# A fixed beat for the maxima's tiles, filter pieces in three spots, edge transposes elsewhere, and last rows asked for early, in a spectral and feed-forward kernel

## The chip, the cores and the metric

The kernel runs on one core of a Trainium2 chip. The core has five engines, each with a queue of its own that is worked off strictly in order: TensorE (PE, matmuls), VectorE (DVE), ScalarE (ACT), GpSimd (POOL) and SyncE (SP). An engine that waits for one instruction waits with everything behind it. DMAs are issued from the queues of SP, ACT and POOL and run on 16 DMA engines. On-chip data lies in SBUF (128 partitions), results of matmuls in PSUM banks. The metric is the device time of one execution in microseconds (us); lower is better.

## The reference

```python
x = A_x                                    # 1 x 2048 x 1024, float32
xn = _layernorm(x, axis=-1)
X = jnp.fft.rfft2(xn, axes=(-2, -1))
s = jnp.fft.irfft2(X * (w_r + 1j * w_i), s=(2048, 1024), axes=(-2, -1))
h = _silu(xn @ w1)                         # w1: 1024 x 3584
g = _silu(h @ w2)                          # w2: 3584 x 1024
return x + s * g
```

The global filter `w_r`, `w_i` is 2048 x 513; the two Fourier transforms are done as matmuls with constant matrices. To keep float32 accuracy on f16 matmuls, every operand is split into a high and a low f16 half, and each product is three matmuls (high·high, high·low, low·high). The splits need a scale, and the scales need maxima of the absolute values of `w1`, `w2`, `w_r` and `w_i`, so each of these is read once for its maximum.

## The kernel before

PE goes through these stages. All positions below are in us from the start of the profiled span.

1. *Plain hidden products* (L601), until 374: `xn @ w1` for the first eight pairs of 128 columns of `w1` (q < 8).
2. *The seven-product part* (L639), 374 to 617: the other six pairs (q = 8 to 13), each for two halves g of the rows, are done by Strassen's scheme. One unit (q, g) is seven products M1 to M7 of 12 matmuls 128x512, 84 products in all. Each product is followed by its evacuation from PSUM. M1, M6, M7 and M4 accumulate one after the other in the same bank, `pa`: between them ACT copies `pa` out (L651 after M1, L653 after M6, L655 after M7), and the next of them can't start on PE before that copy. M3 of a unit stands between M1 and M6 of the next.
3. *The second matrix* (L745 to L747, bank `pb`), from 617 on: seven products m = 0 to 6, each in eight parts j = 0 to 7 of 42 or 21+21 matmuls. The Fourier stages stand between them: forward (`fx`, L1200 to L1202, 16 steps u = 0 to 15), the edge column (`eps`, L1341 to L1343: nine groups of small f32 matmuls that transpose and reverse, 18 records), the filter, inverse (L1467, L1496). For m = 6 each part j finishes rows of the output: DVE L805 and L806 add the stored partial sums, ACT applies silu, L819 and L820 form s·g + x (`finish_out`), and a DMA stores it.

*What sets the order.* The program is written out by hand in one order by Python generators, and each `yield` marks the end of a slot. After every product, `after()` first writes the evacuation of the product before, then runs one slot each of `wq` (`weights1`, w1's maxima and splits), `xq` (`w2max_gen`), `yq` (`wmax_gen`) and up to three slots of the background queue `bg`, which holds the Fourier stages. So an empty `yield 0` in one of these moves what follows it by one product. What a slot writes goes into the in-order queues of SP, ACT, DVE and POOL.

In the seven-product part three streams look for maxima, all fed by DMAs on SP:

- `weights1`: the two tiles of a pair of w1 columns (`r`, L405, 512 KB each) are loaded, and some slots later ACT sums their absolute values (`magnitude`, L289). Then comes the split into f16 halves (ACT L267, DVE L270).
- `w2max_gen`: w2 tiles (`xn`, L469). ACT takes the magnitude of the even tile, DVE subtracts its two halves (L481), SP stores the difference to DRAM (`ws`, L483), and ACT takes the odd tile. In this part it has two spots in the buffer X1; a spot that a store reads can be loaded again only once the store has landed.
- `wmax_gen`: 36 pieces 128x456 of `w_r` and `w_i` (L1133) in two spots, each reduced by DVE to a maximum (L1126). The load of piece k waits for the reduce of piece k − 2.

*The edge.* `f_gen` calls the generator `edge_gen` step by step. Its first step has POOL copy the edge column into order (12 copies, L1334 to L1337), the second does the `eps` matmuls. `eps` takes a buffer from the ring "ft" of two PSUM buffers that also holds `fx`; `pb` goes through the ring "ff" of four banks (`pf`).

*The last rows.* For m = 6, `load_parts` (L738) loads the two stored partial sums of part j (`pd`), and `acc` asks by `rows_for` (L759) for four pieces 128x512: the two halves of s (`sd`) and of x. They are asked for when part j has been written, and used one part later; the last eight pieces (parts 6 and 7) are asked for after PE's part 6.

Of the kernel before, what the change touches and what calls it, by code (L numbers as in the profile page):

```python
# [10 lines left out]
F32 = mybir.dt.float32  # L11
# [8 lines left out]
NFT = F // 128  # L20
# [121 lines left out]
def spectral_ffn(ctx, tc, x, w_r, w_i, w1, w2, ca, kc, ci, tw, pm, out):  # L142
# [29 lines left out]
    def small(name, n=1):  # L172
        return sm.tile([128, n], F32, name=name)
# [113 lines left out]
    def magnitude(raw, out):  # L287
        for k in range(2):
            nc.scalar.activation(junk, raw[:, 512 * k:512 * k + 512], AF.Abs, accum_out=out[:, k:k + 1])  # L289

    def weights1():
# [105 lines left out]
        for q in range(NPL, NP):  # L397
# [7 lines left out]
                    nc.sync.dma_start(r[i], w1v[:, :, (2 * q + i) * 128:(2 * q + i + 1) * 128])  # L405
            else:
                r = early
            yield 0
            yield 0
            yield 0  # L410
            for i in range(2):
                magnitude(r[i].rearrange("p a b -> p (a b)"), ma[:, 2 * i:2 * i + 2])
                yield 0
# [45 lines left out]
    def w2max_gen():  # L459

        tiles, state = {}, [0, 0]

        def load():
            n = state[0]
            if n < NFT and n - state[1] < aux[1] and not (hold_x[0] and n % 2 == 0):
                tiles[n] = aux[0].tile([128, 2, 512], F32, name=f"w2m{n}", tag="x", bufs=4)
                for k, h in enumerate(((0, 1), (1, 0))[n % 2]):
                    f = (n & -2) + k
                    nc.sync.dma_start(tiles[n][:, k], w2[f * 128:(f + 1) * 128, h * 512:(h + 1) * 512])  # L469
                state[0] += 1  # L470
            live_x[0] = state[0] - state[1]

        for n in range(0, NFT, 2):
# [254 lines left out]
    rows = {}  # L728
    READS = ((), (), (), (), (1, 0), (), (2, 0))

    def load_parts(m, j):
# [386 lines left out]

    def wmax_gen():

        mt, tl = small("mw", 36), []
        spots = Map({"y": [(R2[0], 72 * KB + 256), (R2[0], 74 * KB + 256)]})

        def reduce():
            k, t_ = tl.pop(0)
            nc.vector.tensor_reduce(mt[:, k:k + 1], t_, axis=AX.X, op=OP.max, apply_absolute_value=True)  # L1126

        for k in range(36):
            if len(tl) == 2:
                reduce()  # L1130
            src = (w_r, w_i)[k // 18].rearrange("(p r) k -> p (r k)", p=128)
            tl.append((k, spots.tile([128, 456], F32, name=f"wm{k}", tag="y")))
            nc.sync.dma_start(tl[-1][1], src[:, 456 * (k % 18):456 * (k % 18 + 1)])  # L1133
            yield 0.6
            if k % 3 == 2:
                yield 0
        yield 0
        while tl:
            reduce()
# [49 lines left out]
    def f_gen():  # L1189
# [56 lines left out]
        for u in range(16):  # L1246
# [73 lines left out]
    def edge_gen():  # L1320
# [15 lines left out]
            g.tensor_copy(r0[:, n, 0], xv[:, n, 0, 0])  # L1336
            g.tensor_copy(r0[:, n, 1:4], xv[:, n, 0, 3:0:-1])  # L1337
        yield 1
        ps = P["t"].tile([128, 1024], F32, name="eps", tag="ft")
        for n in range(3):  # L1340
            nc.tensor.matmul(ps[:, n * 32 + 8:n * 32 + 32], perm[:, 0], rv[:, n, 1:4].rearrange("m q a r -> m (q a r)"), start=True, stop=True)  # L1341
            nc.tensor.matmul(ps[:, n * 32:n * 32 + 8], perm[:, 1], rv[:, n, 0].rearrange("m a r -> m (a r)"), start=True, stop=False)
# [290 lines left out]
    with tc.manual_schedule():  # L1633
# [168 lines left out]
        for n, (m, j, k) in enumerate(steps):  # L1802
# [77 lines left out]
```

## Time and profile before

| | us |
|---|---|
| three runs | 1300.14, 1294.84, 1294.86; median 1294.86 |
| the profiled execution | 1292.91 |
| its span | 1291.1 |
| PE busy | 1242.7 (96%) |
| DVE / ACT / POOL busy | 991.6 / 567.6 / 279.3 |
| L639, the seven-product part: 1008 matmuls | first at 374.18, PE idle before them 17.4 |
| last stage from 617.19 | 673.9 |

In the profile, a row names line, engine, operation and tiles (out<-in). A row "PE fx L1200 <- DVE xn L1295: 2.9, 1, 2.9" says that PE's instructions of line 1200 that write `fx` waited 2.9 us in all, in one wait, 2.9 us the longest, until DVE's instruction of line 1295 that writes `xn` was done. In a row of the timeline, "x12" merges 12 like instructions, the brackets hold the idle time before them and its releaser. "SPq" is SP's queue of DMA issues. A window's row lists the busy time and the count of each engine in turn, then the granted clock of TensorE (1.00 is full speed), the DMA engines' busy share and GB/s.

### The profile page before, as it was taken

Reading aid. Unit: us, or ns where it says so; the run is one execution under the profiler, and the core shown is the slowest. Engines: PE = TensorE matmul, PEld = TensorE weight load, DVE = VectorE, ACT = ScalarE, POOL = GpSimd, SP = SyncE. Lnnn points to the kernel's source line nnn. Section 1 sums busy time; section 2 is a strip of 40 time slices with the busy share of each in tenths; the row PEclk is TensorE's granted clock in tenths of the full one; section 3 lists DMA queues with packets and bytes.
Section 4 is the critical chain, followed back from the end, with each engine's and each line's share of the span. In section 5 each row is a group of like instructions: output and inputs, shape, how many; then the busy total and the mean of one; then the engine's idle time right before and its main releaser. Section 6 shows DMA issues by size and latency. Waiting matters only on the chain.

```text
span 1291.1 us, 18582 instructions
## 1 busy us (share of the span) xinstructions
PE 1242.7 (96%) x6827; PEld 643.3 (50%) x6827; DVE 991.6 (77%) x1628; ACT 567.6 (44%) x844; POOL 279.3 (22%) x428
## 2 busy tenths in 40 slices
PE   8999999999998988999999999999979999999996
PEld 5544444444443433444445455555544456566654
DVE  6678998899986776785478949996798347886774
ACT  4854575655456676755333223332323222422211
POOL 1211242533441222312300000202125200110011
PEclk9999999999999898999999999999989999999998
DMA  7569697858578788837855788989999988888587
GB/s 241 128 160 231 160 313 204 257 139 216 131 201 230 253 248 277 243 89 239 284 176 184 225 272 200 312 239 301 216 298 266 356 314 321 290 294 283 188 288 233
DMA packets 181595, 306.68 MB, mean 238 GB/s; under 512 B 31744, under 2 KB 89856, under 8 KB 180352
## 3 DMA queue, kind: packets, MB, share of 16 engines
q1 hardware_dynamic: 135584, 163.85, 42.1%
q0 software_dynamic: 30128, 92.82, 25.4%
q10 hardware_dynamic: 15792, 48.83, 10.7%
q8 instruction: 53, 0.87, 0.3%
q14 instruction: 38, 0.31, 0.1%
HBM read 204.25 MB, written 111.67 MB: 245 GB/s over the span
## 4 chain that ended last, share of the span: by engine, by line
PE 50%; DMA 10%; DVE 6%; issue 4%; ACT 3%; POOL 1%; SPq 0%; ACTq 0%; DVEq 0%; POOLq 0%
PE pb L745 11%; PE pb L746 11%; PE pb L747 11%; PE pa L639 5%; DMA r<-in_B_w_dram 3%; PE id L1496 3%; PE iu L1467 3%; PE pe L639 2%; DMA xn<-in_B_w_dram 2%; DMA ws<-xn 1%; DMA r<-in_A_w_r_dram 1%; PE pc L639 1%; PE fx L1200 1%; DMA hd_one<-hoone 1%; ACT both L289 1%
## 5 line engine op out<-in xcount | busy, mean ns | idle before, releaser
L601 PE MATMUL pa<-xn,w 128*128 128x512 f16 x1536 | 335.4, 380 | 5.8 <-DVE w L270 2.4
L745 PE MATMUL pb<-r,w 128*128 128x512 f16 (+1 forms) x798 | 300.3, 376 | 0.0
L746 PE MATMUL pb<-r,w 128*128 128x512 f16 (+1 forms) x798 | 300.0, 376 | 0.0
L747 PE MATMUL pb<-r,w 128*128 128x512 f16 (+1 forms) x798 | 300.0, 376 | 0.0
L601 PEld LDWEIGHTS <-w 128*128 128x128 f16 x1536 | 150.2, 98 | 186.9 <-issue 4.2
L639 PEld LDWEIGHTS <-w 128*128 128x128 f16 x1008 | 100.1, 99 | 142.9 <-issue 27.7
L747 PEld LDWEIGHTS <-w 128*128 128x128 f16 x798 | 78.2, 98 | 91.7 <-issue 1.0
L639 PE MATMUL pa<-r,w 128*128 128x512 f16 x432 | 105.7, 397 | 17.4 <-ACT h L655 8.3
L745 PEld LDWEIGHTS <-w 128*128 128x128 f16 x798 | 78.4, 98 | 85.7 <-issue 0.6
L746 PEld LDWEIGHTS <-w 128*128 128x128 f16 x798 | 78.2, 98 | 85.7 <-issue 0.6
L267 ACT ACTIVATE r<-r,sc 128x512 f16<-128x512 f32 x88 | 61.0, 715 | 99.8 <-DMA r<-in_B_w_dram 64.5
L270 DVE SCALAR_TENSOR_TENSOR r<-r,sc 128x512 f16<-128x512 f32 x88 | 64.5, 744 | 33.2 <-ACT r L267 33.2
L685 POOL DMA_DIRECT2D hd_one<-hoone x52 | 47.2, 907 | 185.1 <-DVE hoone L270 88.9
L685 POOL DMA_DIRECT2D hd_sum<-hosum x52 | 42.5, 924 | 158.8 <-DVE hosum L270 90.0
L270 DVE SCALAR_TENSOR_TENSOR hoone<-h,hs,hoone 128x2048 f16<-128x2048 f32 x28 | 65.7, 2346 | 8.0 <-ACT hoone L267 8.0
L267 ACT ACTIVATE hoone<-h,hs 128x2048 f16<-128x2048 f32 x28 | 55.9, 1995 | 15.6 <-DMA hd_one<-hoone 10.1
L267 ACT ACTIVATE hosum<-hr,hs 128x1536 f16<-128x1536 f32 x28 | 43.9, 1569 | 28.1 <-DVE hr L692 21.3
L611 ACT ACTIVATE h<-pa,ep 128x512 f32<-128x512 f32 x64 | 43.1, 676 | 29.4 <-PE pa L601 27.6
L270 DVE SCALAR_TENSOR_TENSOR hosum<-hr,hs,hosum 128x1536 f16<-128x1536 f32 x28 | 50.7, 1812 | 4.8 <-ACT hosum L267 4.8
L1200 PE MATMUL fx<-xn 128*128 128x256 f16 x192 | 44.6, 278 | 4.4 <-DVE xn L1295 2.9
L691 DVE TENSOR_TENSOR hr<-h 128x1024 f32<-128x1024 f32 x28 | 34.1, 1219 | 18.9 <-ACT h L611 14.0
L1496 PE MATMUL id<-xn 128*128 128x256 f16 x384 | 44.5, 273 | 0.0
(288 smaller groups left out, 2049.6 us busy)
## 6 DMA issues: line engine op xcount, KB each, us to landing
w<-hd_dif ACTq DMA_DIRECT2D x32, 448.0 KB, 7.3
r<-in_B_w_dram SPq DMA_DIRECT2D x56, 256.0 KB, 8.3
w<-hd_sum ACTq DMA_DIRECT2D x32, 448.0 KB, 5.8
w<-hd_one ACTq DMA_DIRECT2D x32, 448.0 KB, 6.7
hd_sum<-hosum POOLq DMA_DIRECT2D x52, 256.0 KB, 5.0
hd_one<-hoone POOLq DMA_DIRECT2D x52, 256.0 KB, 4.6
hd_dif<-hoone POOLq DMA_DIRECT2D x52, 256.0 KB, 4.3
xn<-in_B_w_dram SPq DMA_DIRECT2D x40, 256.0 KB, 4.3
```

What stands on the lines that cost most here:

```text
L267: nc.scalar.activation(hi, raw, AF.Copy, scale=scale)
L270: nc.vector.scalar_tensor_tensor(lo, raw, scale, hi, op0=OP.mult, op1=OP.subtract)
L601: nc.tensor.matmul(ps, w[:, wh, d], xt[:, xh, d], start=(n == 0), stop=(n == 23))
L611: nc.scalar.activation(hq[:, 2 * (c % 2) + f % 2], ps, AF.Silu, scale=ep[:, q:q + 1])
L639: nc.tensor.matmul(ps, lhs(d, wh), rhs(d, xh), start=(name in ("M1", "M5") and d + n == 0), stop=(d + n == 5), skip_group_check=True)
L685: defer(1, lambda k=k, m=m: stores[0].dma_start(hd[m, g][:, :, q].rearrange("f p h s -> f p (h s)"), o[:, k].rearrange("f p h s -> f p (h ...
L745: nc.tensor.matmul(ps, hh[:, 0], w[:, 0], start=first, stop=False)
L746: nc.tensor.matmul(ps, hh[:, 0], w[:, 1], start=False, stop=False)
L747: nc.tensor.matmul(ps, hh[:, 1], w[:, 0], start=False, stop=last)
L1200: nc.tensor.matmul(o, k[:, c, kh, 1], v[:, c, vh], start=(n == 0), stop=False)
L1467: nc.tensor.matmul(ps[:, q], lhs, rhs, start=(n == 0 and r == 0), stop=(n == 2 and r == 1))
L1496: nc.tensor.matmul(o, us[g][:, uh, 2 * p + r], C["ci"][:, ch, g, r], start=(n == 0 and r == 0), stop=(n == 2 and r == 1))
```

## The change

Five edits, in the order of the diff:

- `weights1`: four empty slots instead of three between the load of a pair's w1 tiles and its magnitudes.
- `w2max_gen`: in the seven-product part (where `aux[1]` is 2) a fixed pattern of six slots a pair: load of the odd tile; magnitude of the even one; subtract; store and magnitude of the odd tile; an empty slot; load of the next even tile. Before, a pair took five slots there, and the next even tile was asked for one slot after the store.
- `wmax_gen`: 54 pieces 128x304 in three spots instead of 36 pieces 128x456 in two. One load in each slot; a piece is reduced two slots after its load, and its spot is loaded again one slot after that.
- The edge: the second step of `edge_gen` from within `f_gen` comes only from u = 14 on, and `eps` takes a bank of the ring "ff".
- `load_rest`, new: as soon as, in m = 6 from j = 4 on, the background queue is empty, all rows and partial sums of the parts after the next are asked for at once, into the free buffer X1. `load_parts` and `acc` then find them there.

```diff
@@ weights1
-            yield 0
-            yield 0
-            yield 0
+            for _ in range(4):
+                yield 0
             for i in range(2):
                 magnitude(r[i].rearrange("p a b -> p (a b)"), ma[:, 2 * i:2 * i + 2])
                 yield 0
@@ w2max_gen
+        def put(n):
+            tiles[n] = aux[0].tile([128, 2, 512], F32, name=f"w2m{n}", tag="x", bufs=4)
+            for k, h in enumerate(((0, 1), (1, 0))[n % 2]):
+                f = (n & -2) + k
+                nc.sync.dma_start(tiles[n][:, k], w2[f * 128:(f + 1) * 128, h * 512:(h + 1) * 512])
...
         for n in range(0, NFT, 2):
-            while n + 1 not in tiles:
+            while n + 1 not in tiles and aux[1] == 4:
                 load()
                 yield 0
-            load()
+            early = aux[1] == 4
+            if early:
+                load()
+            elif n not in tiles:
+                put(n)
+                yield 0
+            if n + 1 not in tiles:
+                put(n + 1)
+                yield 0
             d_, o_ = tiles.pop(n), tiles.pop(n + 1)
-            magnitude(d_.rearrange("p a b -> p (a b)"), w2m[:, 2 * n:2 * n + 2])
+            size(n, d_)
             yield 0
             nc.vector.tensor_tensor(d_[:, 0], d_[:, 0], d_[:, 1], op=OP.subtract)
             yield 0.7
             nc.sync.dma_start(ws[n // 2], d_[:, 0])
-            yield 0
-            magnitude(o_.rearrange("p a b -> p (a b)"), w2m[:, 2 * n + 2:2 * n + 4])
-            state[1] += 1
-            load()
-            if aux[1] == 2:
+            if early:
                 yield 0
-            state[1] += 1
-            load()
-            load()
+            size(n + 1, o_)
+            state[1] += 2
+            if early:
+                load()
+                load()
+            else:
+                yield 0
+                yield 0
+                if n + 2 < NFT:
+                    put(n + 2)
             yield 0
@@ load_rest (new), load_parts
+    room = Map({k: [(X1, a * KB + 2 * KB * i) for i in range(n)] for k, a, n in (("rows", 24, 12), ("pt", 48, 6))})
+
+    def load_rest(j):
+        if bg_done[0] or not tdone[0] or queues["bg"]:
+            return
+        bg_done[0] = True
+        while deferred:
+            tick(False)
+        for i in range(j, 8):
+            c, p = 2 * (i // 4), i % 4
+            for _, h in FINALS[6]:
+                if (c, p, h) not in rows:
+                    rows[c, p, h] = rows_for(c, p, h, room, (("rows", 12), ("rows", 12)))
+            for k in READS[6]:
+                if (k, i) not in part:
+                    part[k, i] = room.tile([128, 512], F32, tag="pt")
+                    nc.sync.dma_start(part[k, i], pd[k, i])
...
     def load_parts(m, j):
+        if (READS[m] or (0,))[0] and (READS[m][0], j) in part:
+            return
@@ wmax_gen
-        for k in range(36):
-            if len(tl) == 2:
-                reduce()
-            src = (w_r, w_i)[k // 18].rearrange("(p r) k -> p (r k)", p=128)
-            tl.append((k, spots.tile([128, 456], F32, name=f"wm{k}", tag="y")))
-            nc.sync.dma_start(tl[-1][1], src[:, 456 * (k % 18):456 * (k % 18 + 1)])
-            yield 0.6
-            if k % 3 == 2:
-                yield 0
...
+        for k in range(57):
+            if k >= 3:
+                nc.vector.tensor_reduce(mt[:, k - 3:k - 2], tl.pop(k - 3), axis=AX.X, op=OP.max, apply_absolute_value=True)
+            yield 0.5
+            if k < 54:
+                src = (w_r, w_i)[k // 27].rearrange("(p r) k -> p (r k)", p=128)
+                tl[k] = view(R2[0], 72 * KB + 256 + 1216 * (k % 3), [128, 304], F32)
+                nc.sync.dma_start(tl[k], src[:, 304 * (k % 27):304 * (k % 27 + 1)])
@@ f_gen
-            if u >= 13:
+            if u >= 14:
                 next(edge, None)
             yield 2.5
@@ edge_gen
-        ps = P["t"].tile([128, 1024], F32, name="eps", tag="ft")
+        ps = pf.tile([128, 512], F32, name="eps", tag="ff")
@@ second matrix
+            if m == 6 and j >= 4:
+                load_rest(j + 1)
             if m == 6 or (m, j) == (5, 7):
                 load_parts(6, (j + 1) % 8)
             after(acc(m, j, banks.pop((m, j))))
```

Three places where the order of instructions moves. The first is SP's queue in the seven-product part, between two stores of w2 halves (`ws_140`, `ws_141`); `in_A_w_r_dram` are filter pieces, `in_B_w_dram` at L469 (L473 after the change) tiles of w2, at L405 of w1. Before:

```order
L483 DMA ws_140<-xn 128x512
L1133 DMA r_2498<-in_A_w_r_dram 128x456
L469 DMA xn<-in_B_w_dram 128x512 x2
L1133 DMA r_2498<-in_A_w_r_dram 128x456
L469 DMA xn<-in_B_w_dram 128x512 x2
L1133 DMA r_2498<-in_A_w_r_dram 128x456 x2
L405 DMA r_2498<-in_B_w_dram 128x8x128 x2
L483 DMA ws_141<-xn 128x512
```

And after, where the lines are L496, L1167, L473 and L405:

```order
L496 DMA ws_140<-xn 128x512
L1167 DMA r_2498<-in_A_w_r_dram 128x304 x2
L473 DMA xn<-in_B_w_dram 128x512 x2
L1167 DMA r_2498<-in_A_w_r_dram 128x304
L473 DMA xn<-in_B_w_dram 128x512 x2
L1167 DMA r_2498<-in_A_w_r_dram 128x304 x2
L405 DMA r_2498<-in_B_w_dram 128x8x128 x2
L1167 DMA r_2498<-in_A_w_r_dram 128x304
L496 DMA ws_141<-xn 128x512
```

The first reload after a store stands two products behind it instead of one, and six filter pieces stand between two stores instead of four.

The second place is PE around the edge's transposes, before the change; `fx_8121` is step u = 14 of the forward transform, and `pb_7` the next part of the second matrix:

```order
L1202 LDWEIGHTS xn
L1202 MATMUL fx_8121<-xn 128x128
L1341 MATMUL eps<-xn 128x24
L1342 MATMUL eps<-xn 128x8
L1343 MATMUL eps<-xn 128x8
L745 LDWEIGHTS w_67
L745 MATMUL pb_7_8193<-r_2498,w_67 128x512
```

After the change (`fx_8285` is step u = 15, and `pb_0` the part behind `pb_7`), the three rows of `eps` standing three times in a row in both kernels:

```order
L1230 LDWEIGHTS xn
L1230 MATMUL fx_8285<-xn 128x128
L1369 MATMUL eps<-xn 128x24
L1370 MATMUL eps<-xn 128x8
L1371 MATMUL eps<-xn 128x8
L783 LDWEIGHTS w_67
L783 MATMUL pb_0_8350<-r_2498,w_67 128x512
```

The transposes moved from behind u = 14 to behind u = 15, with the 42 matmuls of `pb_7` and all of u = 15 now ahead of them.

The third place is the end of SP's queue, in m = 6, from the partial sums of part 6 on (`pl_6`, `pd_6`); `sd_1` and `fs_1`, `fx_1` are the rows of part 5, `sd_2` those of part 6, `sd_3` of part 7. Before:

```order
L738 DMA pl_6_2_10883<-pd_6_118 128x512
L738 DMA pl_6_0_10885<-pd_6_102 128x512
L759 DMA fs_1_1_10887<-sd_1_129 128x512
L759 DMA fx_1_1_10889<-in_A_x_dram 128x512
L759 DMA fs_1_0_10891<-sd_1_129 128x512
L759 DMA fx_1_0_10893<-in_A_x_dram 128x512
L738 DMA pl_7_2_10948<-pd_7_119 128x512
L738 DMA pl_7_0_10950<-pd_7_103 128x512
L759 DMA fs_2_1_10952<-sd_2_130 128x512
L759 DMA fx_2_1_10954<-in_A_x_dram 128x512
```

After, from the partial sums of part 6 on (the rows `sd_2` of part 6 stand just ahead of these):

```order
L763 DMA xn<-pd_6_118 128x512
L763 DMA xn<-pd_6_102 128x512
L797 DMA xn<-sd_3_131 128x512
L797 DMA xn<-in_A_x_dram 128x512
L763 DMA xn<-pd_7_119 128x512
L763 DMA xn<-pd_7_103 128x512
L797 DMA fs_1_1_10929<-sd_1_129 128x512
L797 DMA fx_1_1_10931<-in_A_x_dram 128x512
L797 DMA fs_1_0_10933<-sd_1_129 128x512
L797 DMA fx_1_0_10935<-in_A_x_dram 128x512
```

The 12 loads of parts 6 and 7 (each pair `sd_3`, `x` stands twice) now come ahead of the four of part 5, which were third in the list before.

More of the change, by code (lines that the diff above doesn't have):

```diff
@@ L464, in load, with size @@
             n = state[0]
[L465 to L469, printed above, removed]
+            if n < NFT and n - state[1] < 4 and aux[1] == 4 and not (hold_x[0] and n % 2 == 0):
+                put(n)
                 state[0] += 1
             live_x[0] = state[0] - state[1]
+        def put(n):
[3 more added lines that the diff above has]
+                nc.sync.dma_start(tiles[n][:, k], w2[f * 128:(f + 1) * 128, h * 512:(h + 1) * 512])
+        def size(n, t_):
+            magnitude(t_.rearrange("p a b -> p (a b)"), w2m[:, 2 * n:2 * n + 2])
         for n in range(0, NFT, 2):
-            while n + 1 not in tiles:
+            while n + 1 not in tiles and aux[1] == 4:
                 load()
                 yield 0
-            load()
+            early = aux[1] == 4
+            if early:
+                load()
+            elif n not in tiles:
+                put(n)
+                yield 0
+            if n + 1 not in tiles:
+                put(n + 1)
+                yield 0
             d_, o_ = tiles.pop(n), tiles.pop(n + 1)
-            magnitude(d_.rearrange("p a b -> p (a b)"), w2m[:, 2 * n:2 * n + 2])
+            size(n, d_)
             yield 0
@@ L729, in spectral_ffn @@
     READS = ((), (), (), (), (1, 0), (), (2, 0))
+    room = Map({k: [(X1, a * KB + 2 * KB * i) for i in range(n)] for k, a, n in (("rows", 24, 12), ("pt", 48, 6))})
[14 more added lines that the diff above has]
+                    nc.sync.dma_start(part[k, i], pd[k, i])
+    bg_done = [False]
     def load_parts(m, j):
+        if (READS[m] or (0,))[0] and (READS[m][0], j) in part:
+            return
         while m == 6 and held.get("pt"):
@@ L1119, in wmax_gen @@
     def wmax_gen():
[L1121 to L1126, printed above, removed]
-        for k in range(36):
-            if len(tl) == 2:
-                reduce()
-            src = (w_r, w_i)[k // 18].rearrange("(p r) k -> p (r k)", p=128)
-            tl.append((k, spots.tile([128, 456], F32, name=f"wm{k}", tag="y")))
-            nc.sync.dma_start(tl[-1][1], src[:, 456 * (k % 18):456 * (k % 18 + 1)])
-            yield 0.6
-            if k % 3 == 2:
-                yield 0
-        yield 0
-        while tl:
-            reduce()
+        mt, tl = small("mw", 54), {}
+        for k in range(57):
[6 more added lines that the diff above has]
+                nc.sync.dma_start(tl[k], src[:, 304 * (k % 27):304 * (k % 27 + 1)])
         m = small("mwx")
```

## The prediction

> **What bounds the kernel now.** I read the page's busy line first, then what PE waits for in its groups of instructions, then its timeline.
>
> ```profile
> span 1291.1 us, 18582 instructions
> PE 1242.7 (96%) x6827; PEld 643.3 (50%) x6827; DVE 991.6 (77%) x1628; ACT 567.6 (44%) x844; POOL 279.3 (22%) x428
> ```
>
> PE is busy for 96% of the span, and the change neither adds nor removes a matmul. So it can gain only what PE waits, what PE loses at a lower clock, and what follows PE's last matmul. The costliest wait of PE's groups in 374 to 618 us is this one (count, busy time and mean ns, then idle time before it and its releasers):
>
> ```profile
> L639 PE MATMUL pa<-r,w 128*128 128x512 f16 x432 | 105.7, 397 | 17.4 <-ACT h L655 8.3 <-ACT pc L651 6.0 <-ACT h L653 3.1
> ```
>
> L639 is the seven-product part: 17.4 us, all of it for ACT to read bank `pa`. PE's timeline shows the undisturbed beat and the four large ones (a row is start, duration, then in brackets the idle time before it and its releaser):
>
> ```profile
> 374.18 2.75 PE L639 MATMUL pa<-xn,w 128*128 128x512 f16 x12
> ...
> 385.86 2.75 PE L639 MATMUL pc<-xn,w 128*128 128x512 f16 x12
> 388.45 2.75 PE L639 MATMUL pa<-r,w 128*128 128x512 f16 x12
> ...
> 404.41 2.75 PE L639 MATMUL pa<-r,w 128*128 128x512 f16 x12 [2.85 <-ACT h L653]
> ...
> 421.95 5.10 PE L639 MATMUL pa<-r,w 128*128 128x512 f16 x12 [4.43 <-ACT pc L651]
> ...
> 457.14 4.44 PE L639 MATMUL pa<-r,w 128*128 128x512 f16 x12 [4.19 <-ACT h L655]
> ...
> 499.76 5.28 PE L639 MATMUL pa<-r,w 128*128 128x512 f16 x12 [4.14 <-ACT h L655]
> ...
> 617.19 0.38 PE L745 MATMUL pb<-r,w 128*128 128x512 f16 x1
> ```
>
> A product takes 388.45 − 385.86 = 2.59 us, so 84 of them take 217.6 us. The part lasts 617.19 − 374.18 = 243.0 us. **25.4 us are lost**: the four large waits are 2.85 + 4.43 + 4.19 + 4.14 = 15.6 us, the small ones the other 1.8, and the last 8.0 is a slower clock, since after the three waits of over 4 us a product takes 4.4 to 5.3 us instead of 2.75.
>
> ACT isn't late from work but from waiting in order. At the third wait, SP's and ACT's timelines read:
>
> ```profile
> 447.69 2.55 SPq L405 DMA_DIRECT2D r<-in_B_w_dram  x2
> 455.13 0.63 ACT L289 ACTIVATE both<-r 128x512 f16<-128x512 f32 x1 [7.26 <-DMA r<-in_B_w_dram]
> 456.51 0.58 ACT L655 ACTIVATE h<-pa 128x512 f32<-128x512 f32 x1
> ```
>
> A magnitude (L289) stands in ACT's queue ahead of the evacuation L655, waits 7.26 us for its w1 tile, and PE waits for L655. The tile was late at its source: its load was issued by SP behind filter pieces, only at 447.69. ACT's and SP's waits from 366 to 605 us say how often:
>
> ```profile
> ACT both L289 <- DMA xn<-in_B_w_dram: 13.3, 8, 4.6
> ACT both L289 <- DMA r<-in_B_w_dram: 12.8, 4, 7.3
> SPq L1133 <- DVE mw L1126: 44.0, 20, 5.8
> SPq L469 <- DMA ws<-xn: 23.9, 7, 5.1
> ```
>
> SP stands 44 us for spots that the reduces haven't freed, and 24 us for a stored half to land before its spot is loaded again. Everything behind is issued late.
>
> **The change part by part.** *The fixed beat of the w1 and w2 tiles, and the filter pieces,* have one answer. Counts: as many tile loads, stores and magnitudes as before; 54 filter pieces for 36, so 18 more DMAs on SP and 18 more reduces on DVE. Landing times in 374 to 530 us (count, KB, median us from issue to landing), the slowest store, from the chain of waits, and the reduce:
>
> ```profile
> xn<-in_B_w_dram SPq DMA_DIRECT2D x38, 256.0 KB, 4.3
> r<-in_A_w_r_dram SPq DMA_DIRECT2D x18, 228.0 KB, 5.5
> r<-in_B_w_dram SPq DMA_DIRECT2D x8, 512.0 KB, 6.8
> ws<-xn SPq DMA_DIRECT2D x9, 256.0 KB, 4.7
> 386.08 8.81 DMA ws<-xn
> L1126 DVE TENSOR_REDUCE mw<-r 128x1 f32<-128x456 f32 x36 | 22.2, 622 | 17.3 <-DMA r<-in_A_w_r_dram 10.4 <-DMA r<-in_A_w_i_dram 6.8
> ```
>
> The new places in time: a store gets two products (5.2 us) until its spot is loaded again instead of one (2.6), against a median of 4.7 us; the tile that is loaded there gets two products until its magnitude, as before, against 4.3; a w1 tile gets three always (7.8 us) instead of two in three rounds of four, against 6.8. A filter piece gets two products until its reduce, and its spot one more until it is loaded again. So the medians now fit where one of them didn't, and SP's 44 us of waiting should go, since a load no longer follows at once on a reduce that DVE has yet to reach. The tails do not all fit. I keep the small waits (1.8) and, an estimate, 3.6 us for late w1 tiles: four of them, each landing in 8.7 us, 1.9 above its median. That leaves 5.4 of 25.4, a **gain of 20**. The upper bound is 24.5, with half the small waits left; the lower is 8, if nothing but the slower clock goes.
>
> The 18 more reduces: a 304-wide one lies between 0.62 × 304/456 = 0.41 us (by width; then 54 cost what 36 did) and 0.62 us (by instruction; 54 × 0.62 − 22.2 = 11.3 us more). I take the middle, +6. The sum of the windows of the part shows what hides it:
>
> ```profile
> sum 243.00, PE 225.57 PEld 100.07 DVE 175.19 ACT 159.38 POOL 65.60; mean PE 25.06 PEld 11.12 DVE 19.47 ACT 17.71 POOL 7.29
> ```
>
> DVE is free for 243 − 175 = 68 us of the part; were that cover gone, up to 11 us would be on the path. The 18 more DMAs cost SP no more than half the 2.55 us of the row at 447.69 each, for two, in which a wait is counted too: 23 us at most, hidden by the 44 us of waits that go.
>
> [...]
>
> *The edge transposes.* They cost what stands between these rows of PE and POOL:
>
> ```profile
> 954.50 0.27 PE L1200 MATMUL fx<-xn 128*128 128x256 f16 x1
> ...
> 960.83 0.40 PE L1341 MATMUL eps<-xn 128*128 128x24 f32 x2 [3.52 <-POOL xn L1334]
> ...
> 964.62 0.60 PE L1343 MATMUL eps<-xn 128*128 128x8 f32 x2 [0.30 <-POOL xn L1337]
> 966.57 0.59 PE L745 MATMUL pb<-r,w 128*128 128x512 f16 x1
> 965.78 0.18 POOL L1337 COPY xn<-xsv 128x6 f32<-128x6 f32 x1
> 966.00:970.00 4.00, 4.00 (x14) 1.85 (x14) 4.00 (x9) 3.04 (x6) 0.77 (x1) 0.57 1.02 280
> ```
>
> From 960.83 − 3.52 = 957.31 to 966.57 PE does nothing but the 18 edge matmuls, 9.3 us. The clock that the waits brought down, 0.57 on the mean of the next 4 us, costs `pb` 1.5 us more: 10.8 in all. In the new order `pb_7` (42 matmuls at 2.59/12 us, 9.1 us) and u = 15 (like u = 14, 957.3 − 954.5 = 2.8 us) stand ahead, so the edge starts near 957.3 + 9.1 + 2.8 = 969.2, after POOL's last copy ends at 965.97. Unwaited it costs PE 2.2 to 4.4 us: the last eight records took 1.95 us at the lower clock, so 18 take 4.4, and about half that at full. I take 3.0: **gain 7.8**, 6.4 to 8.6. The move into the `pf` ring (4 banks) frees `fx` from a bank held by `eps`; it costs nothing as long as the `pb` in that bank has been read, which is over 9 us earlier.
>
> *The last rows.* 12 loads move ahead of the four of j = 5; none is added. The end by the chain of waits (its DMA), PE's and DVE's timelines, the page's slices and a window:
>
> ```profile
> 1277.03 8.02 DMA fx<-in_A_x_dram
> 1281.09 0.27 PE L747 MATMUL pb<-r,w 128*128 128x256 f16 x1
> 1254.10 0.69 DVE L805 TENSOR_TENSOR pl<-pl,pb 128x512 f32<-128x512 f32 x1 [3.20 <-PE pb L747]
> 1273.43 0.75 DVE L819 SCALAR_TENSOR_TENSOR pl<-fs,s_sc,pl 128x512 f32<-128x512 f32 x1
> 1285.49 0.41 DVE L805 TENSOR_TENSOR pl<-pl,pb 128x256 f32<-128x256 f32 x1
> 1287.85 0.42 DVE L820 TENSOR_TENSOR pl<-pl,fx 128x256 f32<-128x256 f32 x1
> GB/s 241 128 160 231 160 313 204 257 139 216 131 201 230 253 248 277 243 89 239 284 176 184 225 272 200 312 239 301 216 298 266 356 314 321 290 294 283 188 288 233
> 1246.00:1251.00 5.00, 5.00 (x25) 2.27 (x24) 4.84 (x9) 1.33 (x2) 1.08 (x2) 1.00 1.00 399
> ```
>
> The last row, asked for at 1277.03, lands at 1285.05, and DVE's last instruction ends at 1288.27. PE's last matmul ends at 1281.36; the last half's work on DVE, from L805 at 1285.49 to 1288.27, is 2.8 us, so if it starts 0.3 us after PE it ends at 1284.5: the most to gain is 3.8. But from 1254.1 on, 22 pieces of 256 KiB now stand in SP's queue to the last of j = 5's, and POOL stores about six: 7.3 MB. At 399 GB/s that is 18.4 us; at 283, the lowest of the six slices ahead of the last three, 25.9. I take the middle, 340 GB/s, 21.6 us. The rows of j = 5 were used at 1273.43, 19.3 us after 1254.1. So DVE starts 2.3 us later on them; the work that it then has is two rows' ends at full width (j = 5, 6; 2.85 each, two pairs of L819 and L820 at 0.75 + 0.69), two at half (1.8) and two pairs L805, L806 (0.75), 10.8 in all without waits, and it ends 32.4 us after 1254.1 instead of 34.2: **gain 1.8**, from 3.8 to a loss of 2.5.
>
> *The sum:* 20 + 7.8 + 1.8 = 29.6. The profiled execution took 1292.91 us, 1.8 outside its span; 1292.9 − 29.6 = 1263.3. The median of the runs, 1294.86, is 1.95 above it, so **1265**.
>
> **The rivals.**
> 1. *Half the stalls stay.* For it: a store took up to 8.8 us to land, and the tile loads wait behind them in SP's one queue; store (4.7) plus load (4.3) already take 9.0 of the 10.4 us, and the stage's transfers are denser by what it runs faster. Against: medians fit. Two of the four large waits (7.8) stay with half of the clock's 8.0, the small ones (1.8) and half the 3.6: 15.4 stay, 10 are gained, 1275.
> 2. *The filter pieces pace the part.* A spot's turn (load, two products, reduce, one product) is 7.77 us, 18 times. If a piece lands and is reduced in L on the mean over such a turn, the part grows by 18 × (L − 7.77): at 9.2 us its gain is gone, at 9.7 the other gains too, and from 10.1 the kernel is slower by 0.5%. At 10.5, the part costs 49 us over its bare 217.6, 1309. For it: 5.5 us is the median of the present pieces, and DVE, in order, holds every evacuation behind a late reduce. Against: the pieces are a third smaller, and 5.5 + 0.6 is under 7.77. [...]
> 3. *The edge still waits or now holds up a `pb`,* since the two rings meet: its 7.8 are lost, 1273. Against: POOL's copies end 3 us ahead of the new place.
> 4. *The change doesn't do what it says:* the order of instructions shows that it does; no chance of its own.
>
> **How the numbers follow.** My forecast 0.62, rival 1 0.20, rival 2 0.08 (0.05 of it past 10.1 us, the rest about level), rival 3 0.10. The low end is all upper bounds together, 24.5 + 8.6 + 3.8 = 36.9: 1258. Rivals 1 and 3 together, with a loss in the last rows, are 1294.9 − 10 + 2.5 = 1287; 1282 leaves that and rival 2 out, about 2 in 10 with what lies under 1258. 0.5% is 6.5 us, about what a measurement of this kernel can tell from no change. Faster by more than that: 0.62 + 0.20 + 0.10 = 0.92, less 0.06 for pairs of rivals that come together, 0.86. Within: 0.08, these and the level part of rival 2. Slower: 0.06.
>
> **What would show it.** PE's timeline: a product each 2.59 us from start to first `pb`, and no wait for the copies of `pa` over 1 us but one; ACT's wait for w1 and w2 tiles from 26 us to under 10; SP's for reduces from 44 to under 15. No idle time before the edge matmuls, and clock 1.00 around them. After PE's end no DVE wait for a row. Wrong if DVE's waits before the reduces grow past 17 us (rival 2), if SP still waits over 12 us for `ws` (rival 1), or if the end comes more than 7 us after PE's last matmul (last rows).

## The result and the profile after

| us | before | after |
|---|---|---|
| median of the runs | 1295.55 | 1275.70 |
| profiled execution | 1292.91 | 1275.51 |
| its span | 1291.1 | 1273.7 |

The ratio of the times is 0.9836, with a 95% interval of 0.9806 to 0.9866: the kernel became 1.6% faster. The forecast was 1265, 2.3% faster, with a range of 1258 to 1282. One of the four runs after the change took 1436.49 us at a granted clock of 0.849, where the other three took 1274.33 to 1275.90 at 0.993 to 0.995, and the ratio leaves it out. The profiled execution gained 17.4 us where the sum said 29.6.

I cut each trace at the same places of PE's timeline. The cuts are the first matmul of the seven-product part, the first `pb`, the start of u = 12 of the forward transform, the end of the edge or of u = 15 (whichever is later), PE's last matmul and the end of the span:

| us | before | after | gained | forecast |
|---|---|---|---|---|
| seven-product part | 243.0 | 230.0 | 13.0 | 20 |
| from `pb` to u = 12 | 309.2 | 313.1 | −3.9 | 0 |
| u = 12 to the edge's end | 53.5 | 42.4 | 11.1 | 7.8 |
| from there to PE's end | 301.5 | 307.9 | −6.4 | 0 |
| behind PE's end | 9.7 | 6.1 | 3.6 | 1.8 |

Two rows belong together. Before, a wait for the forward transform stood behind u = 12, and after it stands ahead of u = 12 (5.0 us for `xn<-vd`). So the second and third rows make 7.2 us together. The trace of before is one execution, and among the kernels with the old edge it has the shortest of these stretches: from the first `pb` to the edge's end it took 362.7 us, the four others below 365 to 368 and those with the new edge 353 to 358.

In the part, the groups of PE's and DVE's instructions (count, busy time, mean ns, then idle time before them and its releasers) and the waits of ACT and SP from 366 to 595 us now read:

```profile
L655 PE MATMUL pa<-r,w 128*128 128x512 f16 x432 | 99.1, 379 | 11.0 <-ACT pc L667 7.5 <-ACT h L669 2.0 <-ACT h L671 1.5
...
L1162 DVE TENSOR_REDUCE mw<-r 128x1 f32<-128x304 f32 x54 | 24.7, 464 | 26.2 <-DMA r<-in_A_w_i_dram 15.5 <-DMA r<-in_A_w_r_dram 10.7
```

```profile
ACT both L289 <- DMA xn<-in_B_w_dram: 10.3, 6, 4.8
ACT hoone L267 <- DVE h L710: 7.6, 5, 3.5
```

```profile
SPq L1167 <- DVE mw L1162: 32.4, 25, 6.0
...
SPq L473 <- DMA ws<-xn: 9.6, 6, 3.1
```

PE's waits in the part fell from 17.4 to 11.0 us, the longest from 4.43 to 2.71, and its mean matmul is back at 379 ns from 397: the slower clock is gone in this trace. The granted clock of the part is 1.00, and 1.00 too in the window from 534 to 538, at the longest wait; before, it was 0.53 to 0.57 in the windows at the three waits of over 4 us, 419 to 427, 457 to 461 and 498 to 505. (In four more traces with the same part, those of after_again, after_no_edge, after_no_rows and after_less_dma below, one wait near 535 us lasted 2.86 to 3.47 us instead of 2.71, and the 12 matmuls behind it took 4.1 to 4.4 us instead of 2.75.) ACT no longer waits for w1 tiles at all (12.8 us before). But DVE waits longer ahead of the reduces than before, 26.2 us instead of 17.3. And PE's largest wait is now for L667, the evacuation of M1. The timelines of DVE, ACT and PE show what stands ahead of one of them:

```profile
522.48 0.47 DVE L1162 TENSOR_REDUCE mw<-r 128x1 f32<-128x304 f32 x1 [1.60 <-DMA r<-in_A_w_i_dram]
...
524.60 1.22 DVE L710 TENSOR_TENSOR h<-h 128x1024 f32<-128x1024 f32 x1
525.85 2.00 ACT L267 ACTIVATE hoone<-h,hs 128x2048 f16<-128x2048 f32 x1 [3.54 <-DVE h L710]
...
529.79 0.62 ACT L289 ACTIVATE both<-r 128x512 f16<-128x512 f32 x1
...
532.35 0.62 ACT L289 ACTIVATE both<-r 128x512 f16<-128x512 f32 x1
...
533.72 0.58 ACT L667 ACTIVATE pc<-pa 128x512 f32<-128x512 f32 x1
534.34 2.75 PE L655 MATMUL pa<-r,w 128*128 128x512 f16 x12 [2.71 <-ACT pc L667]
```

ACT itself waits for no DMA here. DVE waited 1.60 us for a filter piece ahead of L710; before that it had been busy for some 15 us, with six more reduces among its work. ACT had to wait 3.54 us for DVE, then works without a pause until 534.3 and comes late to L667. PE started M6 at 534.34, 2.71 us late.

At the edge, PE's timeline shows the nine groups without a wait, 957.60 to 959.58:

```profile
957.60 0.35 PE L1369 MATMUL eps<-xn 128*128 128x24 f32 x2
...
959.36 0.37 PE L1371 MATMUL eps<-xn 128*128 128x8 f32 x2
959.58 0.38 PE L783 MATMUL pb<-r,w 128*128 128x512 f16 x1
```

That is 1.98 us in place of 10.8. Behind it, waits of PE have come that the kernel before didn't have:

```profile
1015.14 0.39 PE L783 MATMUL pb<-r,w 128*128 128x512 f16 x1 [1.01 <-DMA w<-hd_one]
1032.03 0.50 PE L1495 MATMUL iu<-xn 128*128 128x256 f16 x3 [0.53 <-POOL xn L1570]
1044.68 1.67 PE L1495 MATMUL iu<-xn 128*128 128x256 f16 x7 [2.70 <-DVE xn L1505]
```

The chain of waits of the same stretch (start, duration, what) runs almost only through transfers:

```profile
958.43 8.83 DMA r<-in_B_w_dram
...
968.43 8.99 DMA r<-in_B_w_dram
...
981.23 7.93 DMA r<-in_B_w_dram
...
989.24 6.10 DMA r<-in_B_w_dram
...
1001.96 9.05 DMA r<-in_B_w_dram
...
1017.53 9.99 DMA xn<-zd
...
1027.59 10.40 DMA pd<-pl
...
1042.73 0.69 DVE pl L832
```

And the windows there (after the busy times: granted clock, DMA share, GB/s) show the DMA engines full:

```profile
945.00:985.00 40.00, 40.00 (x229) 20.97 (x227) 38.88 (x67) 16.16 (x32) 13.01 (x22) 1.00 0.98 311
1000.00:1032.00 32.00, 30.49 (x141) 13.44 (x139) 8.85 (x15) 6.27 (x11) 4.23 (x15) 1.00 1.04 370
1044.00:1048.00 4.00, 3.32 (x16) 2.40 (x17) 2.89 (x8) 1.35 (x2) 0.00 (x0) 0.58 1.05 357
```

### The profile page after: what moved, and what is told of

It is laid out like the page before. It is cut to its first block, busy times and chain, and to the rows that moved or that the text cites. A ratio compares the mean times of both kernels' runs of the same rounds, so it can differ in the third digit from the quotient of the medians.

```text
span 1273.7 us, 18601 instructions
## 1 busy us (share of the span) xinstructions
PE 1234.6 (97%) x6827; PEld 640.0 (50%) x6827; DVE 992.1 (78%) x1646; ACT 565.9 (44%) x844; POOL 269.9 (21%) x428
## 5 line engine op out<-in xcount | busy, mean ns | idle before, releaser
L655 PE MATMUL pa<-r,w 128*128 128x512 f16 x432 | 99.1, 379 | 11.0 <-ACT pc L667 7.5
L701 POOL DMA_DIRECT2D hd_sum<-hosum x52 | 42.7, 932 | 158.1 <-DVE hosum L270 101.7
L267 ACT ACTIVATE hoone<-h,hs 128x2048 f16<-128x2048 f32 x28 | 55.9, 1995 | 21.7 <-DMA hd_one<-hoone 12.2
L267 ACT ACTIVATE hosum<-hr,hs 128x1536 f16<-128x1536 f32 x28 | 44.0, 1570 | 28.6 <-DVE hr L708 23.9
L1495 PE MATMUL iu<-xn 128*128 128x256 f16 x384 | 46.2, 279 | 3.2 <-DVE xn L1505 2.7
```

What stands on the lines that cost most here:

```text
L267: nc.scalar.activation(hi, raw, AF.Copy, scale=scale)
L655: nc.tensor.matmul(ps, lhs(d, wh), rhs(d, xh), start=(name in ("M1", "M5") and d + n == 0), stop=(d + n == 5), skip_group_check=True)
L701: defer(1, lambda k=k, m=m: stores[0].dma_start(hd[m, g][:, :, q].rearrange("f p h s -> f p (h s)"), o[:, k].rearrange("f p h s -> f p (h ...
L1495: nc.tensor.matmul(ps[:, q], lhs, rhs, start=(n == 0 and r == 0), stop=(n == 2 and r == 1))
```

## The experiments

The runs of the kernel before lay higher on some chips (medians 1294.9 to 1297.7), so I compare ratios to the runs beside them, and stretches of the traces. The table holds all experiments: the stretches named above, in us, with "pb–u12" for the first `pb` to u = 12, "u12–edge" for u = 12 to the edge's end, and "to PE's end" from there. There is one trace of each.

| run | ratio, 95% interval | part | pb–u12 | u12–edge | to PE's end | behind |
|---|---|---|---|---|---|---|
| before | 1 | 243.0 | 309.2 | 53.5 | 301.5 | 9.7 |
| after | 0.9836 (0.9806 to 0.9866) | 230.0 | 313.1 | 42.4 | 307.9 | 6.1 |
| only_beat | 0.9884 (0.9867 to 0.9901) | 231.3 | 311.6 | 54.4 | 301.5 | 9.2 |
| only_pieces | 0.9946 (0.9929 to 0.9964) | 240.0 | 313.3 | 51.6 | 301.5 | 8.7 |
| only_edge | 0.9939 (0.9918 to 0.9959) | 241.9 | 312.6 | 43.2 | 308.2 | 6.3 |
| only_rows | 0.9979 (0.9962 to 0.9995) | 242.8 | 315.3 | 52.3 | 301.5 | 6.5 |
| after_no_edge | 0.9883 (0.9845 to 0.9920) | 231.3 | 313.2 | 54.3 | 301.5 | 7.2 |
| after_no_rows | 0.9877 (0.9842 to 0.9912) | 232.3 | 313.7 | 43.6 | 307.4 | 8.4 |
| after_six_pieces | 0.9787 (0.9752 to 0.9822) | 224.1 | 310.2 | 42.7 | 307.5 | 6.1 |
| after_less_dma | 0.9786 (0.9746 to 0.9826) | 233.3 | 314.3 | 41.6 | 301.5 | 6.1 |
| after_again | 0.9844 (0.9826 to 0.9863) | 233.7 | 311.7 | 43.1 | 309.5 | 6.1 |
| late_w1 | 0.9841 (0.9826 to 0.9857) | 228.7 | 311.8 | 42.7 | 310.0 | 6.1 |
| at_once | 0.9830 (0.9806 to 0.9853) | 227.3 | 314.0 | 44.0 | 308.0 | 6.4 |
| both_tuned | 0.9815 (0.9791 to 0.9838) | 226.4 | 309.9 | 45.3 | 305.8 | 6.1 |

The five kernels with the part unchanged from "after" (after, after_again, after_no_edge, after_no_rows, after_less_dma) have it at 230.0 to 233.7 us, so a difference in the part counts only outside these.

**Each part of the change alone.** The edits are those of the diff above, one group at a time; a few of their lines stand for each.

only_beat:

```diff
-            yield 0
-            yield 0
-            yield 0
+            for _ in range(4):
+                yield 0
...
-            magnitude(d_.rearrange("p a b -> p (a b)"), w2m[:, 2 * n:2 * n + 2])
+            size(n, d_)
...
+                if n + 2 < NFT:
+                    put(n + 2)
```

> The kernel before with the new beat of the w1 and w2 tiles alone; filter pieces, edge and last rows as before. Theory 1 (the gain of the seven-product part comes from the beat, and the smaller pieces in three spots hold DVE up: DVE's wait ahead of the reduces grew from 17.3 to 26.2 us): 11 to 16 us faster than before, PE's waits for the copies of pa under 11 us. Rival (the beat needs the three spots, since SP still stands 44 us for reduces ahead of the tile loads): 0 to 6 us faster, SP's wait for reduces stays over 40 us and magnitudes still wait over 15 us for tiles.

The part fell by 11.7 us with the old pieces, ACT's waits for w1 tiles were gone, and the ratio stands for 15 us: theory 1 holds here, though SP still waited 49 us for reduces. PE's waits were 11.6 us against a bound of 11. DVE waited 20.4 us for the old pieces.

only_pieces:

```diff
-        mt, tl = small("mw", 36), []
+        mt, tl = small("mw", 54), {}
...
+                tl[k] = view(R2[0], 72 * KB + 256 + 1216 * (k % 3), [128, 304], F32)
```

> The kernel before with the filter pieces alone: 54 of 128x304 in three spots, one load a product. Theory 1 (the beat gains, the pieces do not): within 4 us of before, DVE's wait ahead of the reduces over 22 us. Rival (the three spots free SP's queue, and that makes the gain): 8 to 13 us faster, SP's wait for reduces falls from 44 to about 32 us.

This lay between the two: 0.5% faster, the part 3.0 us shorter. DVE's wait ahead of the reduces was the longest of all:

```profile
L1124 DVE TENSOR_REDUCE mw<-r 128x1 f32<-128x304 f32 x54 | 24.6, 463 | 31.2 <-DMA r<-in_A_w_i_dram 17.4 <-DMA r<-in_A_w_r_dram 13.5
```

It is 31.2 us, while SP's wait for reduces fell to 20.9. Both theories had half of it: the third spot frees SP and holds DVE. Together with the beat the pieces add little (231.3 to 230.0 us, inside the spread).

only_edge:

```diff
-            if u >= 13:
+            if u >= 14:
...
-        ps = P["t"].tile([128, 1024], F32, name="eps", tag="ft")
+        ps = pf.tile([128, 512], F32, name="eps", tag="ff")
```

> The kernel before with the edge's transposes alone moved and in the other ring. The transposes themselves should take 2 us of PE without a wait instead of 10.8 with their clock. Theory 1 (the stretch behind, which moves 310 to 396 GB/s, is bound by its transfers and gives the gain back): 2 to 5 us faster, with new waits of PE between 1010 and 1060 us of 3 us or more. Rival (the new waits of the changed kernel there come from something else in it): 8 to 9 us faster, no new wait of PE behind.

The traces agree with theory 1: 10.3 us less from u = 12 to the edge's end, 6.7 us more behind it, with waits for the inverse of 2.3 and 1.6 us and 0.8 for a hidden tile. The end behind PE was 6.3 us instead of 9.7, which neither expected, and the stretch ahead of u = 12 was 3.4 us longer, so that the spans of the two traces differ by 3.1 us. The ratio stands for 8 us, more than theory 1 allowed. Where the rest comes from is not shown; the traced execution of before, 1292.91 us, is faster than all 12 of its runs beside this one (1293.92 to 1300.71).

only_rows:

```diff
+    def load_rest(j):
...
+        if (READS[m] or (0,))[0] and (READS[m][0], j) in part:
+            return
...
+            if m == 6 and j >= 4:
+                load_rest(j + 1)
```

> The kernel before with the early last rows alone. Theory 1 (the end behind PE's last matmul shrinks from 9.7 to 6.1 us, as in the changed kernel): 3 to 4 us faster, nothing else moves. Rival (the end was shorter there only because the parts before it ran otherwise): under 1.5 us faster, or slower, with DVE waiting for rows of part 5.

The end shrank from 9.7 to 6.5 us, so theory 1 holds for the end; the ratio stands for 2.7 us, just under its 3 to 4. But the rival's sign came too: in DVE's timeline the rows of part 5 were late, more than the 2.3 us of the prediction:

```profile
1276.62 0.75 DVE L841 SCALAR_TENSOR_TENSOR pl<-fs,s_sc,pl 128x512 f32<-128x512 f32 x1 [5.87 <-DMA fs<-sd]
```

It cost at most 0.4 us of the end (6.5 against 6.1 in the changed kernel), as DVE then worked through with a single wait, of 0.24 us for ACT.

**Parts of the change undone.** after_no_edge:

```diff
-            if u >= 14:
+            if u >= 13:
-        ps = pf.tile([128, 512], F32, name="eps", tag="ff")
+        ps = P["t"].tile([128, 1024], F32, name="eps", tag="ft")
```

> The changed kernel with the edge's transposes put back. Theory 1 (the transfers behind the edge give most of its gain back, and the end is as short without it thanks to the early rows): 2 to 5 us slower than the changed kernel, so 16 to 18 us faster than before; the edge's own stretch some 9 us longer, the stretch from the edge to the last inverse matmul some 6 us shorter, no wait of PE for the inverse. Rival (the edge's gain is kept whole): 8 to 9 us slower than the changed kernel.

The stretch to the edge's end grew by 11.9 us and the one behind shrank by 6.4 to the bare 301.5. Net 5.5 us by these stretches, just above theory 1's 2 to 5 and well under the rival's 8 to 9. By the ratios it is 0.9883 against 0.9836, some 6 us, with intervals that just overlap. PE didn't wait for the inverse, as theory 1 said. The end was 7.2 us, not quite as short as in the changed kernel.

after_no_rows:

```diff
-            if m == 6 and j >= 4:
-                load_rest(j + 1)
```

> The changed kernel without the early last rows. Theory 1 (with the edge moved the last eight rows land in time by themselves, since the end behind PE's last matmul was 6.3 us with the edge alone): within 1 us of the changed kernel, end 6.0 to 6.5 us. Rival (the early rows make the short end): 2.5 to 3.6 us slower than the changed kernel, end over 8.5 us.

Theory 1 falls: the end was 8.4 us, just under the rival's 8.5, and DVE waited for the last rows again. By the ratios the kernel is some 5 us slower than the changed one (0.9877 against 0.9836), with intervals that overlap; 2.3 us of that is the end. Why the end was as short as 6.3 in only_edge stays open. In every run with the early rows it is 6.1 to 7.2 us.

after_six_pieces (the maximum of the filter is taken over 6 of 54 pieces):

```diff
-            if k >= 3:
+            if 3 <= k < 9:
...
-            if k < 54:
+            if k < 6:
...
-        nc.vector.tensor_reduce(m, mt, axis=AX.X, op=OP.max)
+        nc.vector.tensor_reduce(m, mt[:, 0:6], axis=AX.X, op=OP.max)
```

> The changed kernel with 6 of the 54 filter pieces; the maximum is taken over those alone, 48 loads and 48 reduces are left out. Theory 1 (DVE, held up by the reduces' waits for pieces, makes ACT late, and so the five waits after M1): the seven-product part falls from 230 to 220 to 223 us, 7 to 10 us faster than the changed kernel. Rival (the magnitudes of w1 stand between the evacuations of M4 and M1 on ACT, whoever is late): the part stays above 226 us, the waits after M1 stay at 5 us or more in all.

The part fell to 224.1 us, 6 to 10 less than with all pieces, though not to 223. PE's waits:

```profile
L655 PE MATMUL pa<-r,w 128*128 128x512 f16 x432 | 99.1, 379 | 5.5 <-ACT pc L667 3.0 <-ACT h L669 1.4 <-ACT h L671 1.1
```

The waits after M1 fell from 7.5 to 3.0, of which one of 1.91 at 492.31 stood as before. DVE's waits for pieces fell to 2.0 us, and ACT's for DVE's L710 from 7.6 to 0.8. So the pieces are the larger share, and the order on ACT has one of its own. The run takes out the pieces as a whole, their loads and reduces with the waits for them, so it doesn't price DVE's waits alone; at_once below comes nearer to that.

after_less_dma (the second blocks of the w2 tiles of m = 5 are not added):

```diff
-            if m in ADDED:
+            if m == 4:
                 nc.gpsimd.dma_start(raw[n], w2_block(m, q, 1), accum_op=OP.add)
```

> The changed kernel without the 14 DMAs that add the second block to the w2 tiles of m = 5 (3.7 MB, most of them in the stretch between the edge and the inverse): that sum is left out of the computation, no other instruction moves. Theory 1 (the stretch is bound by its transfers): the waits of PE for the inverse and for hidden tiles between 1010 and 1050 us (1.0, 0.5 and 2.7 us, and 1.7 us of slower clock) go, 4 to 6 us faster than the changed kernel. Rival (the waits come from the order, the inverse standing too early behind the edge's last steps on POOL): within 1.5 us of the changed kernel.

All of PE's waits between 1010 and 1050 us are gone, and the stretch from the edge's end is 301.5 us, the bare time of the kernels without the new edge. By the ratios the kernel is some 7 us faster than the changed one (0.9786 against 0.9836 and 0.9844), a little more than expected. Theory 1 holds: without these transfers the 6.4 us are gone. The run doesn't separate two ways in which they act. Without them fewer bytes are moved, and ACT, in order, no longer waits for the summed tiles ahead of the forward transform's last splits (in the changed kernel 10.62 us for one, up to 999.25): the store of `zd` was issued at 995.54 instead of 1001.40, the load of it at 1010.43 instead of 1017.53, though the edge ended 3.4 us later than in the changed kernel.

**What is left of the part's loss.** after_again is the changed kernel once more, beside the next three:

> The changed kernel itself, as the measure for the three beside it on the same chip. All theories: 18 to 22 us faster than before, the seven-product part 230 to 232 us, the end 6 to 6.5 us.

The ratio came out as expected. The part was at the end of its spread, 233.7 us, with one wait of 3.45 us at 536.10 and the slower clock behind it: the mean matmul into `pa` took 384 ns instead of 379.

late_w1:

```diff
-            for _ in range(4):
+            for _ in range(5):
                 yield 0
             for i in range(2):
                 magnitude(r[i].rearrange("p a b -> p (a b)"), ma[:, 2 * i:2 * i + 2])
                 yield 0
-            yield 0
```

> The changed kernel with the two w1 magnitudes one product later (five empty slots ahead of them, one fewer behind), so that one pair of them stands behind the evacuation of M1 instead of ahead of it. Theory 1 (what is left of the part's loss is ACT's backlog ahead of that evacuation, 1.35 us of it this pair): the waits after M1 that now are 1.6, 1.9 and 2.7 us fall by 1 to 1.4 us each, the part by 3 to 5 us. Rival (DVE sets when ACT gets there, and the order on ACT doesn't matter): the part stays within 1 us of the changed kernel's.

Against after_again, the wait of 1.9 us fell to 0.6 and the last from 3.5 to 2.0 us, but the first rose from 1.4 to 2.3; the part was 228.7, 1.3 to 5 us less than the unchanged ones. The whole time did not move measurably. Theory 1 for two of three waits, inconclusive in the sum.

at_once:

```diff
-            yield 0.5
             if k < 54:
                 ...
                 nc.sync.dma_start(tl[k], src[:, 304 * (k % 27):304 * (k % 27 + 1)])
+            yield 0.5
```

> The changed kernel with a filter piece's spot loaded again in the same slot in which it is reduced, so that a piece has three products until its reduce instead of two. Theory 1 (DVE's 26 us of waits for pieces make half of the loss left): DVE's waits ahead of the reduces fall under 15 us, the part by 2 to 4 us. Rival (SP, which then stands at each piece until DVE has reduced, asks for the w1 and w2 tiles later): SP's waits for reduces rise over 45 us, ACT's waits for tiles over 15 us, and the part is no shorter or longer.

```profile
L1162 DVE TENSOR_REDUCE mw<-r 128x1 f32<-128x304 f32 x54 | 24.6, 464 | 9.4 <-DMA r<-in_A_w_i_dram 5.5 <-DMA r<-in_A_w_r_dram 3.7
```

Both signs came. DVE's waits fell from 26 to 9.4 us and the part to 227.3, 2.7 to 6.4 us less than the unchanged ones, as theory 1 said; ACT's waits for L710 fell to 0.8 us. SP's waits for reduces rose to 58.8 us and ACT's for w2 tiles to 17.4, as the rival said, but the part was shorter, against the rival. How much of the gain went back by the tiles is not shown. The whole time did not move measurably (0.9830 against 0.9844).

both_tuned holds the edits of late_w1 and at_once:

> Both of these edits together. Theory 1 (two separate shares of the loss left): the part falls to 222 to 226 us, 4 to 7 us faster than the changed kernel. Rival (one and the same backlog): no faster than the better of the two alone.

The part came to 226.4 us, just outside theory 1's range and 0.9 less than the better one alone, so the rival fits better: mostly one backlog. Its ratio is the lowest of the kernels that compute everything, 0.9815, though its interval overlaps that of the changed kernel beside it. Against the kernel before, it is faster by 1.6 to 2.1%.

## Why the prediction was right, and where it was off

The time lies in the range, but 10.7 us above the point forecast. The range reached beyond 1275 and 1273 to take in rival 1 or rival 3, and neither came; what came instead happened to cost in all about what rival 1 would have. In that measure it was luck. The profiled execution is 12.2 us above its forecast: 7.0 of the part, 6.4 behind the edge and 3.9 ahead of u = 12, less 3.3 at the edge and 1.8 at the end.

*What bounds the kernel:* right. Only PE's waits, its slower clock and the end moved. PE's busy time fell by 8 us with the same 6827 matmuls; the mean granted clock was 0.993 instead of 0.985.

*The part, 20 forecast, 13.0 and 9.3 measured in two traces.* The mechanism held: only_beat shows that the beat makes nearly all of it, and most of the clock came back (a mean matmul into `pa` of 379 and 384 ns in these traces, 397 before). ACT's wait for tiles fell to 10.3 us, near the forecast 10, but SP's for reduces only to 32.4, where under 15 was forecast, and five waits of PE for the copies of `pa` were over 1 us, where one at most was forecast. Two terms were mis-sized. The 3.6 us for late w1 tiles cost nothing: the wait for them fell to zero. In their place stands a term that I had costed at nothing, the filter pieces. I counted the 18 more reduces by their busy time (+6; measured 24.7 − 22.2 = +2.5), and said that DVE's 68 free us hide them. I also wrote that the medians fit, though the row above it had 5.5 us for the pieces of `w_r`, then a half larger, against the 5.2 us that a piece gets. But what pieces cost is the time that DVE waits for one with everything queued behind it: 17.3 us became 26.2, with two products, 5.2 us, for a piece that landed in 5.1 and 4.7 on the median. DVE's delay comes to ACT (3.54 us in the timeline), from ACT to L667, and from there to PE. after_six_pieces puts the price of all pieces at 6 to 10 us; in at_once, with every piece still loaded and reduced but DVE's waits cut to 9.4 us, 2.7 to 6.4 us of it went, though the whole time did not move measurably. It is not a price of the smaller size: only_beat, with the old pieces and 20.4 us of DVE's waits, has the same part (231.3 us), with 6.8 us of ACT's waits for L710. The forecast left out that pieces of either size would still cost PE something once the tiles came in time. This is rival 2's mechanism at a fraction of its price, and the sign that the prediction named for it, DVE's waits past 17 us, came. The smaller pieces landed hardly sooner than the large ones, 5.1 and 4.7 us for 152 KB against 5.5 and 4.5 for 228 KB.

*The edge, 7.8 forecast.* The step itself was right and slightly larger: 10.8 − 2.0 = 8.8, as the transposes came out at the low end of 2.2 to 4.4 us or just below. What failed is that nothing was charged behind it. I checked POOL's copies and the rings, but not what the stretch behind can keep up with. There the DMA engines were full before the change already, as a window of the kernel before shows:

```profile
1015.00:1045.00 30.00, 30.00 (x141) 13.62 (x139) 4.83 (x8) 3.71 (x6) 0.26 (x1) 1.00 1.03 396
```

In the kernel before, PE still came through there without a wait; I take it that the 10 us lost at the edge were what let the transfers keep up, which no run shows by itself. 6.4 us of the gain went back, and after_less_dma shows that they come back when 14 of the transfers are left out.

*The last rows, 1.8 forecast, 3.6 measured,* inside its bounds. The late rows of part 5 were the mis-sized term: in the changed kernel they were not late, and where they were (only_rows, 5.9 us) it changed the end by under half a microsecond. The early rows are not all of the 3.6 us: taking them out lengthens the end by 2.3 us (after_no_rows), and the edge alone gave a short end too (only_edge), for a reason that stays open.

*The rivals.* Rival 1's time, 1275, was met, but not its mechanism: the store of w2 halves does not pace the part, as SP's waits for `ws` fell from 23.9 to 9.6 us. Rival 3 did not come: `eps` did not wait, and no `pb` waited for its bank.

## What to carry to other kernels

Price an instruction that waits for a DMA on an in-order engine by what stands behind it, not by its own duration, and don't count on free time of that engine to hide it: in the changed kernel DVE was free for 54 of the part's 230 us, and the filter pieces still cost PE 6 to 10 us. When a stall on the bounding engine goes, look whether the next stretch is full of transfers: here, at a DMA share of 0.98 to 1.05, PE arrived earlier and waited 1.01, 0.53 and 2.70 us where it had not waited before. Parts that gain alone need not add: here the beat and the pieces gave 11.7 and 3.0 us of the part alone, and 13.0 or less together.

## What was unexpected of the hardware

How long PE waited did not decide alone whether the clock fell. Behind a wait of 2.86 us at 534.66 in after_no_edge it was 0.57, behind one of 3.26 us at 517.77 in both_tuned it was 1.00, in these windows (the third number from the end is the granted clock):

```profile
534.00:538.00 4.00, 3.34 (x9) 1.18 (x9) 2.66 (x10) 1.97 (x7) 3.82 (x7) 0.57 1.00 346
```

```profile
518.00:522.00 4.00, 4.00 (x20) 1.84 (x19) 3.46 (x5) 1.69 (x6) 0.00 (x0) 1.00 1.06 347
```

What decided it besides the length, no run here shows.
